# Where the last step of a leftover layer norm stands on VectorE, at the seam between attention and MLP of a one-core transformer kernel

## The chip, the core and the metric

The kernel runs on one core of a Trainium2 chip: TensorE (PE in the profile; PEld for its weight loads), VectorE (DVE), ScalarE (ACT), GpSimd (POOL) and SyncE (SP), which issues the DMA transfers. The engines run side by side, each through a queue of its own in order. The metric is the device time of one execution in microseconds (us). Lower is better. Line numbers (L1119) are those of the kernel's source as the profile shows them.

## The reference

A block of a transformer with adaptive layer norms. The input x has 2048 tokens of 512 channels, in bfloat16.

```python
mod = (silu(c) @ w_mod).reshape(c.shape[0], 6, 1, -1)
sa, ca, ga, sb, cb, gb = (mod[:, i] for i in range(6))
h = layernorm(x) * (1 + ca) + sa
x = x + ga * A(h, wqkv, wo)
h = layernorm(x) * (1 + cb) + sb
x = x + gb * B(h, w1, b1, w2, b2)
return x

def A(x, wqkv, wo):
    # 32 heads of 16 channels; a token sees itself and the 255 before it
    q, k, v = heads(x @ wqkv)
    p = softmax(where(mask, q @ k.T * 16 ** -0.5, -1e9))
    return (p @ v).merge_heads() @ wo

def B(x, w1, b1, w2, b2):
    # an MLP over the tokens, not the channels: w1 is 2048 x 1792
    h = layernorm(x)
    u = gelu(einsum('bsd,sf->bdf', h, w1) + b1)
    y = einsum('bdf,fs->bds', u, w2) + b2
    return y.transpose(0, 2, 1)
```

What matters for this change: between the attention and the MLP every token passes two layer norms in a row (the one with `cb` and `sb`, and the MLP's own). The MLP multiplies over tokens, so its first product sums over all 2048 of them.

## The kernel before

The tokens are cut into 16 blocks of 128 (`tb` or `sc`, 0 to 15), which form four groups of four (`tg`). `xres[tb]` holds a block of the residual stream in SBUF, 128 tokens by 512 channels, and `hb[tb]` the twice-normed block that the MLP reads.

**Attention and what runs beside it.** A loop over units of scores (L1009) fills most of the time: TensorE makes scores, ScalarE takes their exponentials, TensorE multiplies them with the values. In the gaps a planner in the kernel's source (`Plan`, `fill`, `run_dense`) places other work at build time, by estimated costs and due times: the projections to q, k and v, the products with `wo` for blocks whose attention is finished (in the written order 11, 8, 9, 10 for the third group), and the first partial sums of the MLP. Everything is inside a hand-ordered region (`tc.manual_schedule`), so the order of emission is the order on each engine.

**Chains.** Work behind a block's `wo` product is a chain: a list of steps, each emitted when `run(chain)` is called. The two norms of a block are the chain of `ln23(tb)` (L696): statistics of x (`bn_stats` on VectorE), mean and variance (`bn_aggr` on VectorE) with three small GpSimd steps that make scale and shift (L217, L220, L224), the first norm, the product with 1 + cb, the sum with sb, statistics again, mean and scale again, and at the end `n3`, the second norm's last step: one `tensor_scalar` (L228) that writes `hb[tb]`. Steps marked `either` may go to VectorE or GpSimd; once `pl.tail` is set they go to VectorE. `fill(until)` (L796) always takes the step that can start first, of those that fit before `until`.

**The end of the loop.** After the last unit (L1048 to L1055) the last attention block is normalised (`norm_out`, `norm_rest`, ending with a transpose on VectorE into `OTd`, L691), and then all steps that chains still hold are emitted. In this program one chain is left at that point, with three steps: the second statistics of one block (L702), its mean and scale (L706 and the three GpSimd steps), and `n3` (L228).

**The tail.** A second hand-ordered region follows (L1109). TensorE first does the sums of the MLP's first product over blocks 0 to 3 for four of the 14 column groups (`sum_up`, L1091, accumulators `pu`). Then, for the last four blocks, 12 to 15:

- `t_wo(tb)` (L1112): four matmuls into a `pa` tile, of which there are two banks, and the residual sum on VectorE, `xres[tb] += pa` (L1119);
- `t1(tb)`: statistics of x on VectorE (L1123, L1125) and three GpSimd steps;
- `t2(tb)`: the first norm on ScalarE (L1133), product and sum on VectorE (L1141, L1142), statistics again;
- `t3(tb)`: the second norm's last step on ScalarE (L1133), which writes `hb[tb]`.

The loop at L1157 emits `t_wo(12)`; `t_wo(13)`, `t1(12)`; `t_wo(14)`, `t1(13)`; and so on. The loop at L1166 then adds blocks 4 to 15 in order, six column groups a block, to the six `pu` accumulators; the weights of blocks 10 to 15 are in `w1b`. After that come the gelus (L1104), the remaining eight column groups (L1187), the second product (L1211) with its bias and gate (L1218), the residual sum and the store. SyncE issues the loads of `w1b` and `w2r` (L1077, L1079) between the two regions.

The lines that the change touches, and the loop of the tail:

```python
        add_chain(norm_rest(NG - 1, ND - 1), pl.dve, first=True)
        finish(pl.chains[0])
        pl.tail, pl.dve = True, pl.dve + 50.0
        while pl.chains:
            fill(pl.dve + 9.0)
...
        for step in range(5):
            if step < 4:
                t_wo(12 + step)
            if step:
                t1(11 + step)
```

Of the kernel before, what the change touches and what calls it, by code (L numbers as in the profile page):

```python
# [28 lines left out]
def kernel(  # L29
# [184 lines left out]
    def rstd_of(mv, n, name, r):  # L214

        ve = small.tile([P, n], DT.float32, name=name + "_ve")
        nc.gpsimd.tensor_scalar(  # L217
            out=ve[:], in0=mv, scalar1=EPS, scalar2=0.0, op0=ALU.add, op1=ALU.add,
        )
        nc.gpsimd.tensor_tensor(out=r, in0=ve[:], in1=mhalf[:, 0:n], op=ALU.pow)  # L220

    def normed(mv, r, b):

        nc.gpsimd.tensor_scalar(  # L224
            out=b, in0=mv[:, 0:1], scalar1=r, scalar2=-1.0, op0=ALU.mult, op1=ALU.mult,
        )
# [30 lines left out]
    class Group:  # L257
# [20 lines left out]
        def run(self, pool):  # L278
            while not self.step(pool):
                pass  # L280
            return self
# [202 lines left out]
    with tc.manual_schedule():  # L484
# [280 lines left out]
        pl = Plan()  # L765
# [5 lines left out]
        def variant(chain):  # L771
            item, at = chain[0][0], chain[1]
            if not isinstance(item[0], tuple):
                return item
            dve, pool = item
            by = not pl.tail and pl.pool + pool[4] < max(pl.dve, at) + dve[1] + PLAN[3]
            f, *rest = pool if by else dve
            return (lambda: f(nc.gpsimd if by else nc.vector), *rest)
# [17 lines left out]
        def fill(until):  # L796

            while True:
                able = []
                for n, chain in enumerate(pl.chains):  # L800
                    at = chain[1]
                    f, cost = variant(chain)[:2]
                    t = max(pl.dve, at) if cost else at
                    if t + cost <= until:
                        able.append((t, n))
                if not able:
                    return
                run(pl.chains[min(able)[1]])
                pl.chains[:] = [c for c in pl.chains if c[0]]
# [241 lines left out]
        add_chain(norm_rest(NG - 1, ND - 1), pl.dve, first=True)  # L1051
        finish(pl.chains[0])
        pl.tail, pl.dve = True, pl.dve + 50.0
        while pl.chains:
            fill(pl.dve + 9.0)  # L1055

    ps_s.release()
    npool.release()
# [32 lines left out]
    def sum_up(fc, s1):  # L1091

        for sc in range(summed[fc], s1):
            nc.tensor.matmul(  # L1094
                pu[fc][:], lhsT=w1_of(sc, fc), rhs=hb[sc][:], start=(sc == done.get(fc, 0)), stop=(sc == NT - 1),
            )
        summed[fc] = max(summed[fc], s1)
# [11 lines left out]
    with tc.tile_pool(name="xp2", bufs=4) as xp2, tc.manual_schedule():  # L1109
        v = {}  # L1110

        def t_wo(tb):  # L1112
            pa = ps_big.tile([P, D], DT.float32, name="pa")
            for g in range(ND):
                nc.tensor.matmul(
                    pa[:], lhsT=OTd[3][g][:, (tb - 12) * P : (tb - 11) * P], rhs=wod[:, g, :],
                    start=(g == 0), stop=(g == ND - 1),
                )
            nc.vector.tensor_tensor(out=xres[tb][:], in0=pa[:], in1=xres[tb][:], op=ALU.add)  # L1119

        def t_stats(src, key):
            st = small.tile([P, nc.vector.BN_STATS_DIM], DT.float32, name="ln2_stats")
            nc.vector.bn_stats(out=st[:], in_=src)  # L1123
            v[key] = xp2.tile([P, nc.vector.BN_AGGR_DIM], DT.float32, name="ln2_mv")
            nc.vector.bn_aggr(out=v[key][:], in_=st[:])  # L1125
            rb = xp2.tile([P, 2], DT.float32, name="ln2_rb")
            v[key, "n"] = rb[:, 0:1], rb[:, 1:2]
            rstd_of(v[key][:, 1:2], 1, "ln2", v[key, "n"][0])
            normed(v[key], *v[key, "n"])

        def t_apply(out, src, key):
            scale, shift = v[key, "n"]
            nc.scalar.activation(out=out, in_=src, func=ACT.Identity, bias=shift, scale=scale)  # L1133

        def t1(tb):
            t_stats(xres[tb][:], (2, tb))

        def t2(tb):
            h2 = hb[tb]
            t_apply(h2[:], xres[tb][:], (2, tb))  # L1140
            nc.vector.tensor_tensor(out=h2[:], in0=h2[:], in1=bc_cb1[:], op=ALU.mult)  # L1141
            nc.vector.tensor_tensor(out=h2[:], in0=h2[:], in1=bc_sb[:], op=ALU.add)  # L1142
            t_stats(h2[:], (3, tb))

        def t3(tb):
            t_apply(hb[tb][:], hb[tb][:], (3, tb))


        gelu0 = xp2.tile([P, 1], DT.float32, name="gelu0")
        nc.scalar.activation(out=gelu0[:], in_=mhalf[:, 0:1], func=ACT.Gelu_apprx_tanh)  # L1150
        for fc in pu:
            if fc not in waiting:
                sum_up(fc, 6 if len(waiting) and set(waiting) & set(fgroups[0]) else 4)
        for fc in waiting:
            sum_up(fc, 4)

        for step in range(5):  # L1157
            if step < 4:
                t_wo(12 + step)
            if step:  # L1160
                t1(11 + step)
        for step in range(6):
            for f, n in ((t2, step), (t3, step - 2)):
                if 0 <= n < 4:
                    f(12 + n)
        for sc in range(4, NT):  # L1166
            for fc in pu:
                sum_up(fc, sc + 1)
# [88 lines left out]
```

## Time and profile before

| | |
|---|---|
| time, median of 3 runs | 252.77 us (251.43 to 253.32) |
| the profiled execution | 251.73 us |
| its span, first to last instruction | 250.0 us |
| TensorE matmuls, busy | 229.4 us (92%) |
| VectorE, busy | 181.1 us (72%) |
| ScalarE, busy | 160.2 us (64%) |
| GpSimd, busy | 108.3 us (43%) |
| mean granted TensorE clock | 0.998 |

The profile is of one execution. Busy shares are averages over stages that have different limits, so they say little about one edit: up to about 160 us ScalarE's exponentials and TensorE share the chain of waits, behind that it is TensorE with short stretches of VectorE. An engine's idle time counts only where the chain of waits runs through it. A timeline row gives the start, the length, the engine, the line, the operation, the tile written and the tiles read, how many instructions are merged in the row, and in brackets how long the engine had been idle and what ended that.

### The profile page before, as it was taken

How to read it: one execution, taken by the hardware profiler on the slowest of the kernel's cores; microseconds unless marked ns; L12 is line 12 of the kernel's file. 1: busy time of each engine (PE TensorE's matmuls, PEld its weight loads, DVE VectorE, ACT ScalarE, POOL GpSimd, SP SyncE). 2: the span in 40 equal slices, each digit the busy share in tenths (PEclk: the TensorE clock that was granted, in tenths of full speed). 3: DMA queues.
4: the chain of work that ended last, by engine and by line, in shares of the span. 5: the costliest groups of instructions: out<-in, count | busy, mean ns of one | idle time of the engine just before them, and what ended most of it. 6: DMA issues, size and time to landing. Idle time of an engine off the chain costs nothing.

```text
span 250.0 us, 8264 instructions
## 1 busy us (share of the span) xinstructions
PE 229.4 (92%) x3547; PEld 119.2 (48%) x3585; DVE 181.1 (72%) x363; ACT 160.2 (64%) x183; POOL 108.3 (43%) x222
## 2 busy tenths in 40 slices
PE   6888897999899999899999999979999999999994
PEld 2543554445445545545545545534444444444443
DVE  5988999988799799989899999869624404150643
ACT  2285999998899999999999999703564400000000
POOL 7325462216748629866878789337600000000000
PEclk9999999999999999999999999999999999999999
DMA  5986994064630255000359300699950000111121
GB/s 177 318 265 161 142 326 153 9 127 83 193 139 5 51 91 88 5 3 3 60 84 335 94 0 5 207 393 414 409 200 0 0 0 21 65 41 43 45 84 43
DMA packets 31977, 30.49 MB, mean 122 GB/s; under 512 B 15940, under 2 KB 26564, under 8 KB 31940
## 3 DMA queue, kind: packets, MB, share of 16 engines
q1 hardware_dynamic: 31940, 29.96, 41.2%
q8 instruction: 28, 0.46, 0.7%
q14 instruction: 9, 0.07, 0.1%
HBM read 22.03 MB, written 2.10 MB: 96 GB/s over the span
## 4 chain that ended last, share of the span: by engine, by line
PE 52%; ACT 23%; DVE 11%; SPq 5%; DMA 4%; issue 2%; POOL 2%; POOLq 0%; DVEq 0%; ACTq 0%
ACT et L639 23%; PE py L1211 19%; PE pu L1094 6%; PE pss L616 5%; PE pu L1187 5%; PE dn L453 4%; PE dn L322 4%; PE dn L345 4%; DMA x<-in_A_x_dram 2%; SPq L369 2%; DVE KT L375 2%; DVE t L667 2%; PE pss L628 2%; DVE ln_stats L236 1%; SPq L123 1%
## 5 line engine op out<-in xcount | busy, mean ns | idle before, releaser
L639 ACT ACTIVATE et<-pss 128x1024 bf16<-128x1024 f32 (+1 forms) x152 | 139.7, 1037 | 6.7 <-PE pss L628 6.2
L1211 PE MATMUL py<-guT,w2r 128*128 128x512 bf16 (+1 forms) x234 | 48.3, 366 | 0.2
L616 PE MATMUL pss<-QT,KT 32*128 32x64 bf16 (+3 forms) x720 | 37.2, 254 | 4.7 <-ACT et L639 1.8
L1211 PEld LDWEIGHTS <-w2r 128*128 128x128 bf16 x238 | 23.3, 98 | 25.3
L1218 DVE SCALAR_TENSOR_TENSOR o<-py,bFM,bc_gb 128x512 bf16<-128x512 f32 (+1 forms) x17 | 11.7, 716 | 30.5 <-PE py L1211 30.5
L345 PE MATMUL dn<-h1T,wqkv 128*128 128x512 bf16 x111 | 31.1, 381 | 1.8 <-issue 1.1
L616 PEld LDWEIGHTS <-KT 32*128 32x128 bf16 x720 | 14.2, 92 | 34.3 <-issue 22.7
L217 POOL TENSOR_SCALAR ln_ve<-ln_mv 128x1 f32<-128x1 f32 (+1 forms) x40 | 9.3, 232 | 43.0 <-DVE ln_mv L237 19.9
L667 DVE STREAM_TRANSPOSE t<-pss 128x512 f32<-128x512 f32 x32 | 20.9, 691 | 4.3 <-PE pss L656 4.3
L656 PE MATMUL pss<-et,VaugT 64*32 64x320 bf16 (+4 forms) x720 | 20.8, 253 | 1.1 <-ACT et L639 0.6
L656 PE MATMUL pss<-et,Vx 64*32 64x320 bf16 (+4 forms) x720 | 20.9, 254 | 0.0
L628 PE MATMUL pss<-mask_rown,mask_hown 32*128 32x128 bf16 (+1 forms) x304 | 20.6, 206 | 0.0
L656 PEld LDWEIGHTS <-VaugT 64*32 64x32 bf16 x720 | 18.7, 91 | 3.8 <-issue 3.3
L683 POOL TENSOR_TENSOR merge<-t,zr 128x512 bf16<-128x512 f32 x13 | 13.8, 1059 | 15.4 <-DVE zr L680 15.3
L628 PE MATMUL pss<-mask_rfar,mask_hfar 32*128 32x64 bf16 (+1 forms) x304 | 19.8, 200 | 0.0
L220 POOL TENSOR_TENSOR ln_rb<-ln_ve,mhalf 128x1 f32<-128x1 f32 x32 | 18.3, 572 | 2.7
L656 PEld LDWEIGHTS <-Vx 64*32 64x32 bf16 x720 | 17.8, 91 | 1.4 <-issue 0.6
L322 PE MATMUL dn<-wqkv,h1T 128*128 128x512 bf16 x58 | 16.0, 380 | 2.0 <-DVE sT_rep L583 0.7
L1102 DVE TENSOR_TENSOR gelu_a<-pu,part 128x512 f32<-128x512 f32 x10 | 6.4, 686 | 13.4 <-PE pu L1187 8.2
L453 PE MATMUL dn<-hb,w1hi 128*128 128x512 bf16 x51 | 14.5, 381 | 0.5 <-issue 0.3
L345 PEld LDWEIGHTS <-wqkv 128*128 128x128 bf16 x120 | 9.6, 97 | 10.7 <-DVE KT L375 0.7
L691 DVE STREAM_TRANSPOSE OTd<-merge 128x512 bf16<-128x512 bf16 x16 | 11.2, 699 | 1.2 <-POOL merge L683 1.2
(130 smaller groups left out, 366.9 us busy)
## 6 DMA issues: line engine op xcount, KB each, us to landing
w2r<-in_B_w_dram SPq DMA_DIRECT2D x14, 512.0 KB, 10.2
wmod<-in_w_mod_dram SPq DMA_DIRECT2D x12, 256.0 KB, 4.7
w1b<-in_B_w_dram SPq DMA_DIRECT2D x6, 448.0 KB, 7.3
Vx<-VaugT SPq DMA_DIRECT2D x16, 147.5 KB, 2.5
x<-in_A_x_dram SPq DMA_DIRECT2D x16, 128.0 KB, 3.6
w1hi<-in_B_w_dram SPq DMA_DIRECT2D x6, 320.0 KB, 4.8
out_dram<-otile SPq DMA_DIRECT2D x15, 128.0 KB, 1.7
wqkv<-in_B_w_dram SPq DMA_DIRECT2D x4, 320.0 KB, 3.9
```

Source lines behind the costliest of these rows:

```text
L220: nc.gpsimd.tensor_tensor(out=r, in0=ve[:], in1=mhalf[:, 0:n], op=ALU.pow)
L322: nc.tensor.matmul(pv[:], lhsT=h1T[tg][:, dc, tl * P : (tl + 1) * P], rhs=wqkv[:, dc, 2 * D : 3 * D], start=(dc == 0), stop=(dc == ND - 1),)
L345: nc.tensor.matmul(pq[:], lhsT=wqkv[:, dc, col0 : col0 + P], rhs=h1T[tg][:, dc, :], start=(dc == 0), stop=(dc == ND - 1),)
L453: nc.tensor.matmul(ps[:], lhsT=w1_of(s0 + n, fc), rhs=hb[s0 + n][:], start=(n == 0), stop=(s0 + n + 1 == s1),)
L616: nc.tensor.matmul(pss[j // 2][:, j % 2, 64 * at : 64 * (at + c1 - c0)], lhsT=Kring[kh // 8 % 3][rows, g8, kh % 8].rearrange("p n t -> p ( ...
L628: nc.tensor.matmul(o[:, at[0] : at[-1] + 1 : step, :], lhsT=mask_h[name][rows].rearrange("p n t -> p (n t)"), rhs=mask_r[name][rows, :].un ...
L639: nc.scalar.activation(out=state["e", tg, g8, ui][:, 2 * a : 2 * a + 2, 0:n], in_=state.pop((u, a))[:, :, 0:n], func=ACT.Exp, scale=SCORE_ ...
L656: nc.tensor.matmul(state["po"][32 * j : 32 * j + 32, par, 64 * c0 : 64 * c1], lhsT=v[:, h * DV : h * DV + 32], rhs=state["e", tg, g8, ui][ ...
L667: nc.vector.transpose(out=state["t2"][:, par, :], in_=state["po"][:, par, :])
L683: eng.tensor_tensor(out=m[:].rearrange("p (b a d) -> p a b d", a=2, d=DH), in0=t2v[:, :, :, 0:DH], in1=zr[:].to_broadcast([P, 2, 16, DH]), ...
L1094: nc.tensor.matmul(pu[fc][:], lhsT=w1_of(sc, fc), rhs=hb[sc][:], start=(sc == done.get(fc, 0)), stop=(sc == NT - 1),)
L1211: nc.tensor.matmul(pys[n][:, c0:c1], lhsT=w2r[:, fc, tb * P : (tb + 1) * P], rhs=guT[fc][:, c0:c1], start=(fc == gelus[0]), stop=(fc == ge ...
```

## The change

The steps of the chains that are left are emitted in turn until each chain holds only its last step. That last step is emitted in the tail, behind `t_wo(12)` and `t_wo(13)` and ahead of `t1(12)`. The tail's mark (`pl.tail`) is set as before, so the step goes to VectorE as before.

```diff
         pl.tail, pl.dve = True, pl.dve + 50.0
-        while pl.chains:
-            fill(pl.dve + 9.0)
+        while any(len(chain[0]) > 1 for chain in pl.chains):
+            for chain in pl.chains:
+                if len(chain[0]) > 1:
+                    run(chain)
...
         for step in range(5):
             if step < 4:
                 t_wo(12 + step)
+            if step == 1:
+
+                for chain in pl.chains:
+                    run(chain)
             if step:
                 t1(11 + step)
```

## The prediction

> **What bounds the kernel now.** I read the chain of waits first, because it names what the end hangs on, then the timeline of each engine between 163 and 185 us, where the edited code runs. The chain's stretch around the edit and its end:
>
> ```profile
> 164.75 0.19 DVE ln_mv L706
> ...
> 165.98 0.28 POOL ln_rb L224
> 166.28 0.41 DVE hb L228
> 166.70 0.61 DVE x L1119
> 167.35 1.89 PE pa L1115 x8
> 169.24 4.10 PE pu L1094 x19
> ...
> 246.36 0.50 DVE o L1218
> 246.88 0.29 DVE otile L1223
> ```
>
> Columns are start, length, engine, tile, line. Up to 167.35 the chain runs through the leftover norm: mean and variance on VectorE (L706), three small steps on GpSimd ending with L224, the norm's last step on VectorE (L228, writing hb), then a residual sum (L1119), and only then TensorE. From 167.35 to 246.36 the chain is TensorE alone: whatever is taken off ahead of 167.35 reaches the end, unless TensorE meets something late on the way.
>
> TensorE there, from its timeline:
>
> ```profile
> 164.55 0.81 PE L1115 MATMUL pa<-wod,OTd 128*128 128x512 bf16 x3
> 165.20 0.59 PE L1115 MATMUL pa<-wod,OTd 128*128 128x512 bf16 x2
> 167.35 1.89 PE L1115 MATMUL pa<-wod,OTd 128*128 128x512 bf16 x8 [1.55 <-DVE x L1119]
> 169.07 0.38 PE L1094 MATMUL pu<-hb,KT 128*128 128x512 bf16 x1
> ```
>
> Each `pa` tile takes four matmuls. The fourth of block 12 starts at 164.55, the eighth (last of block 13) ends at 165.20 + 0.59 = 165.79. There are two `pa` banks, so block 14 has to wait until block 12's sum has emptied one: 1.55 us of idle. And VectorE:
>
> ```profile
> 166.28 0.41 DVE L228 TENSOR_SCALAR hb<-hb,ln_rb 128x512 bf16<-128x512 bf16 x1 [1.35 <-POOL ln_rb L224]
> 166.61 0.68 DVE L1119 TENSOR_TENSOR x<-pa,x 128x512 bf16<-128x512 f32 x1
> 167.21 0.68 DVE L1119 TENSOR_TENSOR x<-pa,x 128x512 bf16<-128x512 f32 x1
> 167.81 0.69 DVE L1123 BATCH_NORM_STATS2 ln_stats<-x 128x6 f32<-128x512 bf16 x1
> 168.70 0.66 DVE L1119 TENSOR_TENSOR x<-pa,x 128x512 bf16<-128x512 f32 x1
> ```
>
> It waits 1.35 us at L228 for GpSimd while both sums stand queued behind; the first could have begun at about 164.95, when L706 is over (164.94) and block 12's matmuls end (164.55 plus a matmul's 0.38, the row of 169.07, is 164.93).
>
> **The change, part by part.** One norm is left over: a single wait of VectorE for GpSimd (L228) lies between the last attention block and the first sum, and it reads and writes hb.
>
> *The loop that replaces `fill`.* With one chain, taking its steps in turn gives the order that `fill` gave: statistics, then mean with the three GpSimd steps. Nothing is added, nothing moved: 0.
>
> *The last step.* It is one VectorE instruction and issues nothing else: no DMA, nothing on GpSimd, SyncE or TensorE. On VectorE it goes behind two sums and stays ahead of the statistics of block 12. No other queue is passed.
>
> *The first sum* now starts when block 12's matmuls are done. In the rows above, a sum that starts at 166.61 and lasts 0.68 ends at 167.29, and TensorE goes on at 167.35: 0.06 from sum to matmul. I take 0.06 for the way there too, so the sum runs from 164.93 + 0.06 = 164.99 to 165.67, and block 14 can start at 165.73. TensorE's own next slot is 165.79 less 0.38 plus the 0.215 between matmul starts (164.55 to 165.20 is three of them), 165.63. So block 14 starts at 165.73 instead of 167.35: 1.62 us earlier; the upper bound is 167.35 − 165.63 = 1.72.
>
> *The second sum* waits for block 13: 165.79 + 0.06 = 165.85, ends 166.53. This wait is new at this place in the queue; behind it stand the norm's last step and everything of blocks 12 to 15. Block 15's matmuls come at 165.73 + 4 × 0.215 = 166.59, and the bank is free at 166.53 + 0.06 = 166.59: just in time, at most 0.1 lost if either row is a little long.
>
> *What stands behind.* The norm's last step has its operands at 165.98 + 0.28 = 166.26, so it waits for nothing now and starts one spacing after the second sum, 165.85 + 0.60 = 166.45 (166.61 to 167.21 is 0.60). Block 12's statistics follow 0.33 later (166.28 to 166.61), at 166.78 instead of 167.81: the VectorE ladder of blocks 12 to 15 moves up by 1.03, less than TensorE's 1.62. The delayed hb belongs to a block of the third group, whose last one, block 10, is the last in the written order, and TensorE takes hb 10 only with the first w1b weights (below), over 8 us later. Holding it back costs 0; without that cover it would cost 0.2, the step's end at 166.86 against 166.69.
>
> *Beside the sums* now run the three GpSimd steps, 165.02 to 166.26, which had VectorE idle. What company does to such steps:
>
> ```profile
> 170.09 0.66 DVE L1119 TENSOR_TENSOR x<-pa,x 128x512 bf16<-128x512 f32 x1
> 170.26 0.22 POOL L217 TENSOR_SCALAR ln_ve<-ln_mv 128x1 f32<-128x1 f32 x1
> ...
> 173.96 0.55 POOL L224 TENSOR_SCALAR ln_rb<-ln_mv,ln_rb 128x1 f32<-128x1 f32 x1
> 174.07 0.39 DVE L1141 TENSOR_TENSOR hb<-hb,bc_cb 128x512 bf16<-128x512 bf16 x1
> ```
>
> Beside a sum from PSUM the step keeps 0.22; beside a product of two SBUF tiles L224 takes 0.55, against 0.28 in the chain. The nearest row is the sum's, so I add 0 and keep doubling as the other end: 1.24 us more would put the last step at 167.50 and leave the ladder where it was, with TensorE's 1.62 untouched by it. The Trainium skill (GPSIMD Engine Reference, Key points) says GpSimd contends with VectorE instructions that run in a two-port mode or have two SBUF inputs. A sum has one SBUF input, so that rule too gives 0 here, where the wider warning that any busy VectorE slows GpSimd would give the 1.24; the two rows side with the narrow wording.
>
> *What TensorE meets next.* It needs hb of blocks 12 to 15 in the last four rounds of six matmuls:
>
> ```profile
> 176.03 0.81 ACT L1133 ACTIVATE hb<-hb,ln_rb 128x512 bf16<-128x512 bf16 x1 [2.32 <-POOL ln_rb L224]
> ...
> 180.88 0.81 ACT L1133 ACTIVATE hb<-hb,ln_rb 128x512 bf16<-128x512 bf16 x1 [0.75 <-POOL ln_rb L224]
> ...
> 176.84 0.38 PE L1094 MATMUL pu<-hb,w1b 128*128 128x512 bf16 x1
> 176.84 7.93 PE L1094 MATMUL pu<-hb,w1b 128*128 128x512 bf16 x35
> ```
>
> The w1b rounds begin with block 10 at 176.84, so block 12 is due 12 matmuls later, 179.4, and block 15 30 later, 183.3. Their hb are ready at 176.84 and 181.69. After the change the needs are 177.8 and 181.7, the hb (1.03 earlier) 175.8 and 180.7: 1.0 us to spare at the tightest; if the ladder did not move at all, 181.69 against 181.7, still no stall. The weights:
>
> ```profile
> L1077 SPq DMA_DIRECT2D w1b<-in_B_w_dram x6: 327/431/432, 157.2 to 159.5; - x6
> DMA to landing us min/median/max: 4.1/7.3/9.3
> ...
> L1211 PEld LDWEIGHTS <-w2r x238: 97/98/98, 197.6 to 245.9; 128*128 128x128 bf16 x119
> L1079 SPq DMA_DIRECT2D w2r<-in_B_w_dram x14: 327/328/802, 160.6 to 176.5; - x14
> DMA to landing us min/median/max: 10.0/10.2/11.5
> ```
>
> w1b has landed by 159.5 + 9.3 = 168.8 at the latest, needed at 175.2; w2r by 176.5 + 11.5 = 188.0, needed at 196.0. Last, the accumulators: the six `pu` banks are released when the last of their six gelus ends, and the second pair of L1187 takes them:
>
> ```profile
> 186.68 0.69 ACT L1104 ACTIVATE guT<-pu,bFM 128x512 bf16<-128x512 f32 x1
> 188.07 1.03 PE L1187 MATMUL pu<-hb,wqkv 128*128 128x512 bf16 x4
> ```
>
> 187.37 against 188.07: 0.7 to spare, and both sides follow TensorE, so the margin moves along whatever order the six take.
>
> **The sum.** −1.62 from the start of block 14, 0 to +0.1 at block 15, 0 elsewhere: −1.6 us. The profiled execution took 251.73 (span 250.0, 1.73 around it) and would take 250.1. That execution is 1.04 under the median of the three runs, 252.77; I put the kernel before at the middle of the two, 252.25, and the kernel after at 252.25 − 1.6 = 250.65, that is 250.7, or 0.64% faster.
>
> **Rivals.**
> *The ladder holds TensorE again.* The idle would reappear ahead of a round of blocks 12 to 15. It decides once the ladder is later than it is now; a full loss of the gain takes 1.6 us of that. For it: GpSimd steps stretched in company, and TensorE gains more than the ladder. Against: 1.0 us to spare after a shift of 1.03. Half the gain lost gives 251.45. Chance 0.06.
> *The clock gives it back and more* (the slower side). From 165.7 on TensorE has no pause:
>
> ```profile
> core 0: us, PE busy (x) PEld busy (x) DVE busy (x) ACT busy (x) POOL busy (x), PEclk, DMA share, GB/s
> ...
> 176.80:184.60 7.80, 7.75 (x36) 3.53 (x36) 2.45 (x6) 4.05 (x7) 2.92 (x8) 1.00 0.97 387
> 184.60:198.00 13.40, 13.35 (x63) 6.07 (x63) 5.16 (x8) 6.78 (x11) 0.00 (x0) 1.00 0.01 4
> 198.00:250.00 52.00, 48.11 (x234) 23.09 (x236) 18.47 (x36) 1.33 (x2) 0.00 (x0) 0.99 0.12 41
> ```
>
> The granted clock (the figure ahead of the DMA share) dips to 0.99 in the last stretch. TensorE's path from 165.7 to 246.4 is about 80 us, so a clock 2% lower costs 1.6 and decides; 0.95 costs 4 and gives 252.25 − 1.6 + 4.0 = 254.7. Against: 13.35 us busy of 13.40 ran at 1.00. Chance 0.07, mostly small.
> *The order on VectorE stays.* If the last step is still put ahead of the sums, nothing changes: 252.25. The block's order is written by hand, so 0.05.
>
> **How the numbers follow.** Forecast 0.82, rivals 0.06, 0.07 and 0.05. Low end: the fastest run 251.43 less the upper bound 1.72, 249.7, with 0.2 for rounding of spacings taken over four to eight matmuls, 249.5. High end: no gain, 252.25, and 0.25 for the run spread, 252.5; it leaves out most of the clock case. A change of 1%, 2.5 us, is about what a measurement here can tell from none; the three runs spread over 1.9. The forecast at 0.64% crosses the bound only by such spread: of its 0.82, 0.16 faster, 0.64 within, 0.02 slower; the ladder 0.06 within; the clock 0.03 within and 0.04 slower; the unchanged order 0.04 within and 0.01 slower. Faster 0.16, within 0.77, slower 0.07.
>
> **What would show it.** Right: VectorE goes L706, L1119, L1119, L228, L1123 with the first sum at about 165.0, no idle of TensorE ahead of the third `pa`, the first `pu` matmul after it at 167.5, w1b at 175.2, block 12's statistics at 166.8, the last matmuls and the span 1.6 earlier. Wrong: TensorE idle in a w1b round (the ladder), a clock under 0.98 (the clock), L228 ahead of the sums (the order), or a first sum that starts well after 165.0.

## The result, and the profile after

The changed kernel takes 250.41 us (median of 22 runs), the kernel before 252.37 (median of 22); the ratio is 0.9929 with a 95% interval of 0.9911 to 0.9947. One of the changed kernel's 22 executions, 254.26 us at a mean granted clock of 0.986, is left out of the ratio, which is worked out from the rest and is not the quotient of the two medians (0.9922). The profiled execution has a span of 248.3 us against 250.0.

The end of the chain of waits of the changed kernel (start, length, engine, tile, line; the tail's lines are two further on than before, those behind it up to six):

```profile
159.06 1.34 PE pss L656 x95
160.40 3.56 PE pu L1096 x16
163.96 3.53 PE pa L1117 x16
167.49 15.54 PE pu L1096 x72
183.03 13.17 PE pu L1193 x61
196.20 48.40 PE py L1217 x238
244.62 0.49 DVE o L1224
245.14 0.29 DVE otile L1229
```

VectorE, GpSimd and the norms are gone from it. From 160.40 to 244.62 the end hangs on TensorE's own work and on nothing else. The timelines of the changed kernel around the edit, VectorE's first, then GpSimd's:

```profile
164.63 0.18 DVE L706 BATCH_NORM_AGGREGATE ln_mv<-ln_stats 128x2 f32<-128x6 f32 x1
164.86 0.69 DVE L1121 TENSOR_TENSOR x<-pa,x 128x512 bf16<-128x512 f32 x1
165.72 0.69 DVE L1121 TENSOR_TENSOR x<-pa,x 128x512 bf16<-128x512 f32 x1 [0.17 <-PE pa L1117]
166.33 0.41 DVE L228 TENSOR_SCALAR hb<-hb,ln_rb 128x512 bf16<-128x512 bf16 x1
166.65 0.69 DVE L1125 BATCH_NORM_STATS2 ln_stats<-x 128x6 f32<-128x512 bf16 x1
```

```profile
164.91 0.22 POOL L217 TENSOR_SCALAR ln_ve<-ln_mv 128x1 f32<-128x1 f32 x1 [1.63 <-DVE ln_mv L706]
165.21 0.56 POOL L220 TENSOR_TENSOR ln_rb<-ln_ve,mhalf 128x1 f32<-128x1 f32 x1
165.87 0.26 POOL L224 TENSOR_SCALAR ln_rb<-ln_mv,ln_rb 128x1 f32<-128x1 f32 x1
```

This execution reaches the edit 0.11 us earlier than the one before (the first `pa` matmul at 163.80 against 163.91), which has to be allowed for in each comparison. The two sums now run while GpSimd makes the norm's scale; of the old 1.35 us wait 0.17 is left, for block 13's matmuls, and the norm's last step waits for nothing: its operands are there at 165.87 + 0.26 = 166.13, it starts at 166.33. TensorE:

```profile
163.80 2.40 PE L1117 MATMUL pa<-wod,OTd 128*128 128x512 bf16 x10
...
165.31 0.67 PE L1117 MATMUL pa<-wod,OTd 128*128 128x512 bf16 x2
...
167.33 1.03 PE L1096 MATMUL pu<-hb,KT 128*128 128x512 bf16 x4
...
175.10 7.93 PE L1096 MATMUL pu<-hb,w1b 128*128 128x512 bf16 x36
182.87 1.03 PE L1193 MATMUL pu<-hb,wqkv 128*128 128x512 bf16 x4
```

The matmul at 165.31 is block 13's last, the next is block 14's first: the row of two ends at 165.98, so the second starts a matmul's 0.38 earlier, at 165.60, with nothing idle in between that the profile marks. The first w1b matmul comes 1.74 us earlier than before, 1.63 without the offset, and the rounds behind it hold no pause: 36 matmuls in 7.93 us, the same time as before (where 35 of the 36 are recorded).

### The profile page after: what moved, and what is told of

Same layout as the page of the kernel before. It is cut to its first block, busy times and chain, and to the rows that moved or that the text cites. A ratio compares the mean times of both kernels' runs of the same rounds, so it can differ in the third digit from the quotient of the medians.

```text
span 248.3 us, 8302 instructions
## 1 busy us (share of the span) xinstructions
PE 232.6 (94%) x3585; PEld 119.2 (48%) x3585; DVE 181.0 (73%) x363; ACT 160.1 (64%) x183; POOL 108.2 (44%) x222
## 4 chain that ended last, share of the span: by engine, by line
PE 56%; ACT 24%; DVE 7%; SPq 5%; DMA 5%; issue 1%; POOL 1%; POOLq 0%; DVEq 0%; ACTq 0%
ACT et L639 24%; PE py L1217 19%; PE pu L1096 8%; PE pss L616 6%; PE pu L1193 5%; PE dn L453 4%; PE dn L322 4%; PE dn L345 4%; DMA x<-in_A_x_dram 2%; SPq L369 2%; PE pss L628 2%; DVE KT L375 2%; DVE ln_stats L236 2%; PE pa L1117 1%; SPq L123 1%
## 5 line engine op out<-in xcount | busy, mean ns | idle before, releaser
L345 PE MATMUL dn<-h1T,wqkv 128*128 128x512 bf16 x120 | 32.6, 381 | 0.5 <-DVE KT L375 0.5
L322 PE MATMUL dn<-wqkv,h1T 128*128 128x512 bf16 x64 | 17.0, 381 | 1.6 <-DVE KT L375 0.9
L453 PE MATMUL dn<-hb,w1hi 128*128 128x512 bf16 x56 | 15.2, 381 | 0.0
L412 PE MATMUL dn<-wod,OTd 128*128 128x512 bf16 x48 | 12.6, 381 | 0.0
```

The costliest lines, as they stand in the source:

```text
L322: nc.tensor.matmul(pv[:], lhsT=h1T[tg][:, dc, tl * P : (tl + 1) * P], rhs=wqkv[:, dc, 2 * D : 3 * D], start=(dc == 0), stop=(dc == ND - 1),)
L345: nc.tensor.matmul(pq[:], lhsT=wqkv[:, dc, col0 : col0 + P], rhs=h1T[tg][:, dc, :], start=(dc == 0), stop=(dc == ND - 1),)
L453: nc.tensor.matmul(ps[:], lhsT=w1_of(s0 + n, fc), rhs=hb[s0 + n][:], start=(n == 0), stop=(s0 + n + 1 == s1),)
```

## The experiments

The runs of one kernel differ by 2 us and more, and in the profiled executions the code ahead of the tail, which is the same in all of them, ends anywhere from 163.8 to 165.1. So besides the ratio I use a yardstick within one execution: from the first `pa` matmul to the end of the span. First `pa` and span are from the one profiled execution of that kernel; each ratio is to executions of the kernel before that were taken alongside (medians 252.37 to 252.40 us). The ladder, as in the prediction, is the run of VectorE steps that belong to the norms of blocks 12 to 15.

| kernel | first pa | span | yardstick | median us | ratio to before, 95% interval |
|---|---|---|---|---|---|
| before | 163.91 | 250.0 | 86.1 | 252.37 | |
| changed | 163.80 | 248.3 | 84.5 | 250.41 | 0.9929, 0.9911 to 0.9947 |
| last step behind one sum | 164.24 | 249.5 | 85.3 | 251.84 | 0.9972, 0.9955 to 0.9989 |
| before, TensorE's idle filled | 164.18 | 249.0 | 84.8 | 250.97 | 0.9942, 0.9915 to 0.9969 |
| before, last step on GpSimd | 165.06 | 249.6 | 84.5 | 250.95 | 0.9939, 0.9918 to 0.9960 |
| ladder back by one instruction | 164.44 | 248.9 | 84.5 | 250.66 | 0.9926, 0.9897 to 0.9955 |
| ladder back by three | 163.97 | 249.2 | 85.2 | 251.17 | 0.9964, 0.9944 to 0.9983 |
| last step behind all statistics of x | 164.39 | 248.9 | 84.5 | 250.41 | 0.9908, 0.9874 to 0.9941 |
| last step behind everything | 165.04 | 253.6 | 88.6 | 253.84 | 1.0072, 1.0037 to 1.0108 |

**Half of the change.** The last step goes between the two sums.

```diff
-            if step == 1:
+            if step == 0:
 
                 for chain in pl.chains:
                     run(chain)
```

> The norm's last step stands behind the first residual sum alone, ahead of the second. Theory (TensorE was starved of its two pa banks by the wait in front of the sums, one bank per sum): block 14's matmuls still follow without idle, but the second sum waits with the last step until about 166.2 and starts at about 166.5, so block 15's matmuls come at about 167.2 instead of 166.5 and TensorE idles some 0.7 us there. From the first pa matmul to the end: 84.5 us in the changed kernel, 86.1 before; here 85.2 to 85.3, so about half of the gain is kept, ratio to the kernel before about 0.996. Rival (what counts is only the first sum, or only how early the ladder of VectorE steps of blocks 12 to 15 starts): no idle at block 15 and 84.5, or a loss of the whole 0.4 us by which the ladder shifts, with the idle in the w1b rounds.

Timelines of VectorE and of TensorE in that kernel:

```profile
165.30 0.69 DVE L1121 TENSOR_TENSOR x<-pa,x 128x512 bf16<-128x512 f32 x1
166.62 0.41 DVE L228 TENSOR_SCALAR hb<-hb,ln_rb 128x512 bf16<-128x512 bf16 x1 [0.63 <-POOL ln_rb L224]
166.95 0.68 DVE L1121 TENSOR_TENSOR x<-pa,x 128x512 bf16<-128x512 f32 x1
```

```profile
164.24 2.83 PE L1117 MATMUL pa<-wod,OTd 128*128 128x512 bf16 x12
167.68 1.02 PE L1117 MATMUL pa<-wod,OTd 128*128 128x512 bf16 x4 [0.62 <-DVE x L1121]
```

Twelve `pa` matmuls now run through, so the first sum frees block 14. Block 15 waits for the second sum behind the last step, 0.62 us. The yardstick is 85.3, 0.8 below the kernel before and 0.8 above the changed kernel: each bank is worth about half, as the theory said. The idle is at block 15 and not in the w1b rounds, which speaks against the rivals.

**TensorE's idle filled, the order on VectorE left as before.**

```diff
         for step in range(5):
+            if step == 2:
+                for fc in pu:
+                    sum_up(fc, 5)
             if step < 4:
                 t_wo(12 + step)
```

> The kernel before, with the norm's last step ahead of both sums, but six of TensorE's later matmuls (block 4 for the six pu column groups) are emitted between block 13's and block 14's pa matmuls. Theory (the gain is TensorE's idle time and nothing else): the sums start at 166.6 as before, block 14 at about 167.35 as before, the idle ahead of it falls from 1.55 to about 0.3 us, the first w1b matmul comes 1.3 us earlier and the ladder stays where it was with 0.35 us to spare; from the first pa matmul to the end 86.1 less 1.3 = 84.8, ratio about 0.995. Rival (the gain comes from the earlier sums and the earlier ladder): TensorE finishes its filler early but waits in the rounds of blocks 12 to 15, 86.1 and a ratio of 1.00.

Timelines of TensorE and of VectorE there:

```profile
165.91 1.03 PE L1094 MATMUL pu<-hb,KT 128*128 128x512 bf16 x4
166.77 0.59 PE L1094 MATMUL pu<-hb,w1hi 128*128 128x512 bf16 x2
167.63 1.89 PE L1115 MATMUL pa<-wod,OTd 128*128 128x512 bf16 x8 [0.26 <-DVE x L1119]
...
175.82 7.93 PE L1094 MATMUL pu<-hb,w1b 128*128 128x512 bf16 x36
```

```profile
166.89 1.28 DVE L1119 TENSOR_TENSOR x<-pa,x 128x512 bf16<-128x512 f32 x2
168.09 0.69 DVE L1123 BATCH_NORM_STATS2 ln_stats<-x 128x6 f32<-128x512 bf16 x1
```

The six matmuls take the idle down from 1.55 to 0.26 and the yardstick to 84.8, 1.3 below before, although the sums start as late as ever and the ladder has not moved: with the 0.27 taken off by which this execution is later, they stand at 166.62 and 167.82, against 166.61 and 167.81. So it was TensorE's idle time that cost, not the lateness of the sums themselves.

**The wait taken out of VectorE's queue, the order of emission left as before.** The last step goes to GpSimd.

```diff
             def n3(eng):
-                apply_norm(eng, hb[tb][:], v["h2"][:], v["n"])
+                apply_norm(nc.gpsimd if pl.tail else eng, hb[tb][:], v["h2"][:], v["n"])
```

> The kernel before, its order of emission, but the norm's last step goes to GpSimd instead of VectorE, so VectorE has no wait for GpSimd in front of the sums. Theory (it is the wait at the head of VectorE's queue that cost, not the place of the step): sums at about 165.0 and 165.8, block 12's statistics at about 166.4, TensorE without idle, 84.5 from the first pa matmul to the end, ratio about 0.993. The step itself takes 0.8 to 1.0 us there and ends at about 167.1, ahead of block 12's first GpSimd step. Rival (GpSimd working in SBUF beside VectorE slows the sums or the statistics): the second sum or the statistics take over 0.8 us instead of 0.69, the ladder moves by less than 1.0 us; TensorE would still lose at most 0.2.

VectorE, GpSimd and TensorE in that kernel:

```profile
166.13 0.69 DVE L1119 TENSOR_TENSOR x<-pa,x 128x512 bf16<-128x512 f32 x1
166.99 0.69 DVE L1119 TENSOR_TENSOR x<-pa,x 128x512 bf16<-128x512 f32 x1 [0.17 <-PE pa L1115]
167.60 0.69 DVE L1123 BATCH_NORM_STATS2 ln_stats<-x 128x6 f32<-128x512 bf16 x1
```

```profile
167.51 0.76 POOL L228 TENSOR_SCALAR hb<-hb,ln_rb 128x512 bf16<-128x512 bf16 x1
168.73 0.22 POOL L217 TENSOR_SCALAR ln_ve<-ln_mv 128x1 f32<-128x1 f32 x1 [0.45 <-DVE ln_mv L1125]
```

```profile
165.06 3.70 PE L1115 MATMUL pa<-wod,OTd 128*128 128x512 bf16 x16
```

All 16 `pa` matmuls run through and the yardstick is 84.5, that of the changed kernel, with the step emitted where it always was and the old loop with `fill` still in place. The cost was the wait at the head of VectorE's queue. The second sum and the statistics keep their 0.69 beside the step on GpSimd, so the rival with slowed VectorE falls; the step itself takes 0.76 us, a little less than the 0.8 to 1.0 expected. (This execution started the tail 1.15 us later than that of the kernel before; hence the later clock times.)

**How much the ladder has to spare.** One statistics instruction of block 9, with an unused result, behind the last step; in the other kernel `range(3)`, three of them.

```diff
                 for chain in pl.chains:
                     run(chain)
+                for _ in range(1):
+                    extra = small.tile([P, nc.vector.BN_STATS_DIM], DT.float32, name="extra")
+                    nc.vector.bn_stats(out=extra[:], in_=hb[9][:])
```

> The changed kernel with one more statistics instruction on VectorE (of block 9, result unused) behind the norm's last step; it puts the ladder of blocks 12 to 15 back by about 0.7 us. Theory (1.1 us to spare): TensorE does not wait, 84.5 us from the first pa matmul to the end, ratio about 0.993. Rival (the ladder sets the end): 85.2, ratio about 0.996.

> The changed kernel with three more statistics instructions on VectorE (of block 9, results unused) behind the norm's last step and ahead of block 12's statistics; nothing else waits for them. They put the ladder of blocks 12 to 15 back by about 2.0 to 2.1 us. Theory (ladder has about 1.1 us to spare in the changed kernel: hb of block 15 ready at 180.5, needed at 181.6): TensorE idles about 1.0 us in the last w1b rounds, 84.5 + 1.0 = 85.5 from the first pa matmul to the end, ratio about 0.997. Rival (the ladder sets the end already): 84.5 + 2.05 = 86.5, ratio 1.00 to 1.002. Rival (more than 2 us to spare): 84.5.

With one, the yardstick stays at 84.5 and the w1b rounds run through:

```profile
175.75 7.93 PE L1096 MATMUL pu<-hb,w1b 128*128 128x512 bf16 x35
```

It moves the ladder by 0.61 and not by the 0.7 expected (block 12's statistics at 167.90, against 166.65 and the 0.64 by which this execution is later). With three, ScalarE's last step for block 15 and TensorE's rounds:

```profile
181.68 0.81 ACT L1135 ACTIVATE hb<-hb,ln_rb 128x512 bf16<-128x512 bf16 x1 [0.75 <-POOL ln_rb L224]
```

```profile
175.27 5.39 PE L1096 MATMUL pu<-hb,w1b 128*128 128x512 bf16 x24
180.98 3.02 PE L1096 MATMUL pu<-hb,w1b 128*128 128x512 bf16 x12 [0.32 <-ACT hb L1135]
```

TensorE stops ahead of block 14 and, since the last twelve matmuls take 3.02 us instead of 11 × 0.216 + 0.38 = 2.75, by another 0.27 ahead of block 15. From the first start to the last end the 36 take 8.73 us instead of 7.93. The yardstick is 85.2 instead of the 85.5 expected: the three instructions start 0.60 us apart, so they put the ladder back by 1.8 and not by 2.0 to 2.1 (block 12's statistics at 168.61, against 166.65 and the 0.17 by which this execution is later). 1.8 less the 0.7 to 0.8 lost leaves 1.0 to 1.1 to spare in the changed kernel. The same from its rows: block 15's hb is written at 179.71 + 0.81 = 180.52 and needed 30 matmuls of 0.216 behind 175.10, at 181.6.

**The last step later still.** Behind the loop of `t_wo` and `t1`; in the other kernel, whose second part follows, behind the loop of `t2` and `t3`.

```diff
-            if step == 1:
-
-                for chain in pl.chains:
-                    run(chain)
             if step:
                 t1(11 + step)
+        for chain in pl.chains:
+            run(chain)
         for step in range(6):
```

```diff
                 if 0 <= n < 4:
                     f(12 + n)
+        for chain in pl.chains:
+            run(chain)
         for sc in range(4, NT):
```

> The changed kernel, but the norm's last step stands behind all four sums and all four statistics of blocks 12 to 15. Theory (hb of block 10 is free until the first w1b round at 175.1, and the ladder is not binding): the statistics of block 12 start 0.33 us earlier, hb of block 10 is written at about 171, TensorE notices nothing, 84.5 from the first pa matmul to the end, ratio about 0.993. Rival (the ladder sets the end, or hb of that block is needed earlier): 0.3 less, or an idle of TensorE ahead of 175.

> The changed kernel, but the norm's last step stands behind all VectorE work of blocks 12 to 15. Theory (block 10 is the leftover block, its first reader is the first w1b round at 175.1): the step ends at about 178.5, TensorE idles about 3.3 us ahead of the first w1b matmul, 84.5 + 3.3 = 87.8 from the first pa matmul to the end, ratio about 1.006. Rival (the leftover block is read later, with block 11 or after): 0.2 to 1.3 less for each round, or an idle in another place.

Behind the four sums and statistics the step costs nothing (84.5; it ends at 171.76, the first w1b matmul is at 175.69). Its ratio of 0.9908 cannot be told from the changed kernel's: the intervals overlap. Behind everything, TensorE and its windows show:

```profile
176.34 1.03 PE L1191 MATMUL pu<-hb,wqkv 128*128 128x512 bf16 x4
179.64 9.62 PE L1096 MATMUL pu<-hb,w1b 128*128 128x512 bf16 x35 [2.27 <-DVE hb L228]
```

```profile
core 0: us, PE busy (x) PEld busy (x) DVE busy (x) ACT busy (x) POOL busy (x), PEclk, DMA share, GB/s
...
177.40:179.60 2.20, 0.00 (x0) 0.00 (x0) 2.01 (x6) 1.24 (x2) 1.49 (x4) 1.00 1.04 413
179.60:183.20 3.60, 3.56 (x9) 1.26 (x9) 0.00 (x0) 1.10 (x2) 0.89 (x3) 0.54 1.03 411
183.20:189.10 5.90, 5.85 (x28) 2.69 (x28) 0.00 (x0) 0.89 (x2) 0.00 (x0) 0.99 0.35 139
```

The first w1b matmul waits for the step (L228), 3.3 us behind 176.34, where it would have stood: the leftover block is read first there, as expected. The yardstick is 88.6, though, not 87.8. Two things were not foreseen. Four matmuls of the next column groups (L1191 at 176.34), which the source has behind the hand-ordered region, ran in the gap, worth 4 × 0.216 = 0.9; that the build's own ordering moved them is likely, but not shown. And behind 2.27 us without a matmul the granted clock (the figure ahead of the DMA share) was 0.54 for 3.6 us: the w1b matmuls take 9.62 instead of 7.93, 1.7 more. 84.5 + 3.3 − 0.9 + 1.7 = 88.6. The 1.7 belong to this execution, the longest of the ten (255.35 us), and not to every one, as the last section shows; without them the yardstick would be 86.9.

## Why the prediction was right

It foresaw 250.7 us, 1.6 us or 0.64% less; measured are 250.41 and 0.71% less, with an interval from 0.53% to 0.89%. The start of that sum, 252.25 us, was chosen between a median of three and one profiled execution; that 252.37 was measured is in part luck. The medians lie 1.96 us apart, the ratio stands for 1.8 and the rows below explain 1.6: the rest is inside the interval and has no shown cause. Step by step, in the profiled executions, with the offset of 0.11 taken off:

- *The first sum* was to start at 164.99; it started at 164.86, or 164.97 in the old execution's time. Block 14's matmuls were to start at 165.73; 165.60, or 165.71.
- *The second sum* at 165.85 (measured 165.83) frees block 15's bank just in time: no idle is marked there. That both banks count, about half each, is shown by the last step between the sums.
- *The last step* at 166.45 (166.44) without a wait, and *block 12's statistics* at 166.78 (166.76).
- *GpSimd beside the sums* was put at no cost: 0.22, 0.56 and 0.26, against 0.22, 0.56 and 0.27 with VectorE idle.
- *What TensorE meets next*: the tightest spare was put at 1.0 us. The changed kernel's rows give 1.1, and the two kernels that put the ladder back bracket it: 0.6 goes free, 1.8 costs 0.7 to 0.8.
- *Holding back hb* was put at nothing under a cover of over 8 us: with the step at 171.4 it is free, behind everything it stops TensorE at the first w1b matmul, which names the reader.
- *The sum* of −1.6 us is the yardstick's 86.1 − 84.5.

Of the rivals, the ladder does not hold TensorE (one instruction more goes free), the order did change on VectorE, and the clock did not give the gain back in the profiled execution: it was 1.00 in the changed kernel's windows from the first `pa` matmul to the last `py` (the tiles of the second product).

```profile
175.10:182.90 7.80, 7.80 (x38) 3.52 (x37) 2.92 (x8) 4.63 (x7) 3.38 (x9) 1.00 1.03 410
182.90:196.10 13.20, 13.20 (x63) 6.01 (x62) 5.16 (x8) 6.73 (x11) 0.00 (x0) 1.00 0.09 37
196.10:244.60 48.50, 48.48 (x239) 23.12 (x237) 17.69 (x34) 1.33 (x2) 0.00 (x0) 1.00 0.12 41
```

The 0.99 of the old kernel's last stretch, on which that rival leaned, was no sign of load: the stretch had been cut at 250.0, past TensorE's last matmul, and windows that end with the matmuls show 1.00.

In single executions of the changed kernel a lower clock does go with a longer time. A stretch like the one in the kernel with the step behind everything, 3.4 us at half clock, lowers the mean granted clock by 0.5 × 3.4 / 250 = 0.007 and costs 1.7 us, as much as the gain. Four of the 22 executions have a mean of 0.993 or less and took 251.92 to 254.26 us; the other 18 have 0.997 or more and took at most 251.15. Of the kernel before, 2 of the 45 executions taken with the experiments show such a mean (253.85 and 254.40 us); of the four other versions in which TensorE waits at most 0.26 us here, none of 29, and of the two that wait longer, without the one behind everything, 1 of 24. What the four executions met is in no trace, and that the change makes it more frequent is not shown.

No version tried beats the changed kernel by more than its interval, and its trace marks no wait of TensorE from 160.40 to 244.62, so nothing is left there for another order of this seam to remove.

## What to carry to other kernels

Where a short chain hops from one engine to another and back, its waiting instruction stands at the head of an in-order queue: look there for work that is ready behind it and whose end frees a buffer that the bottleneck waits for, and put that work ahead, move the waiting step to another queue, or give the bottleneck other ready work (here worth 1.6, 1.6 and 1.3 us). What may be held back, and for how long, is read from its first reader, and how far the next stage can slip from the time at which each of its results is needed. A TensorE wait may cost more than its length when the clock falls behind it (in one execution here, 1.7 us behind a pause of 2.27).

## What was not expected of the hardware

In the profiled execution of the kernel with the step behind everything, a pause of TensorE of 2.27 us (177.37 to 179.64) was followed by a granted clock of one half: the windows from 180 to 183 us show 0.50, and about 1.7 us were lost in the w1b rounds. Pauses of 1.55 us (the kernel before) and 0.62 us (the step between the sums) left it at 1.00, in one execution each. The Trainium skill (TensorE: Matmul & The Clock Gate, Part 1) says that the clock drops to half after at least one idle window of about 3.4 us and that the window runs freely. The depth and, at about 3.4 us, the length of the slow stretch agree; the pause ahead of it here was shorter than one window.

The length of the pause alone does not decide. Behind the last matmul of the kernel before (it ends at 246.32) the clock is 1.00 up to 248.8 and 0.50 from 249.2 on, so it fell some 2.5 us into the idle time; behind the last matmul of the changed kernel (244.58) it is still 1.00 when the span ends, 3.7 us later. And of the ten executions of the kernel with the step behind everything, four have a mean granted clock of 1.00 (252.19 to 253.82 us), which a stretch of 3.4 us at half clock would have taken to 0.993. That fits a window that runs freely, so that its phase counts, but no run here shows the phase.
